# LN roots and the identity matrix moved between engines, and chord sets halved, in an attention and gated-MLP kernel

## The chip, the cores and the metric

One core of a Trainium2 chip runs the whole program. The metric is the time of one execution on the device in microseconds (us), lower is better. A unit in this text is one block of 128 x 512 attention scores; there are 2048.

In the profile PE is TensorE, PEld its weight loads, DVE is VectorE, ACT is ScalarE, POOL is GpSimd. "L1233" is line 1233 of that kernel's source; the line numbers of two kernels differ.

## The reference, cut to what matters

```python
B, S, D, H, F = 1, 2048, 512, 32, 1792
def _layernorm(x): return (x - mean(x)) / sqrt(var(x) + 1e-5)
def _A(x):                                   # attention, 32 heads of 16
    q, k, v = split(x @ wqkv)
    p = softmax(einsum("bhqd,bhkd->bhqk", q, k) / 4)
    return merge(einsum("bhqk,bhkd->bhqd", p, v)) @ wo
def _B(x): return (sigmoid(x @ w_gate) * (x @ w_up)) @ w_down
h = x + _A(_layernorm(x))                    # LN1
out = h + _B(_layernorm(h))                  # LN2
```

## The kernel before

The instruction order of every engine is fixed when the kernel is built. A Python scheduler keeps a model clock for each engine, with assumed durations, and places each piece of work where the model says that it is ready. The rows of x come in 16 tiles of 128, in four chunks of four. Layer normalization needs the reciprocal root of each row's variance, called *root* here; GpSimd takes it with its power operation. The first exps start as soon as chunk 0 is through LN1 and its projections; the other twelve row tiles and the dense projections run beside the attention.

A score tile has three units (two in the first stretch). ACT computes exp on two of them; the third can be taken by DVE, which writes an int16 approximation of the exp's bits. That one needs two more int16 copies, shifted by a constant (the *chords*), and all three are multiplied with V. So a split moves one unit's exp from ACT to DVE, and costs PE two more products with V (*value products*). The chords are int16 additions packed four to a 64-bit word, which GpSimd does. Units of DVE are collected in a set, in one buffer J of three planes: set size `GQ`, buffers `QB`. Sets of four are called quads below, sets of two pairs.

```python
nc.vector.memset(eps_t[:], 1e-5)
nc.scalar.activation(out=A0[:], in_=eps_t[:], func=ACT.Exp)       # loads the exp table
nc.vector.memset(fill[:], 1.0)
make_identity(nc, ident_bf[:])                                    # memset and select on GpSimd
nc.gpsimd.memset(Vaug[:, :, :, DH:VW], 0.5)                       # the sum column of V
... mask, ident2, maskz from ident_bf, on VectorE ...

def rstd_of(dst, var, eps=1e-5):                                  # LN1, every row tile
    v = small.tile([P, 1], FP32, name="nv")
    nc.gpsimd.tensor_scalar(out=v[:], in0=var, scalar1=eps, scalar2=None, op0=ALU.add)
    nc.gpsimd.tensor_tensor(out=dst, in0=v[:], in1=power[:], op=ALU.pow)

def early_ln(c):                                                  # chunks 1 to 3
    for i in range(TQ):
        j = ... statistics of the row tile, on VectorE ...
        j = rstd_job(rstds[c][:, i:i + 1], mvs[c][:, i, 1:2], j)  # on GpSimd
        ja.append(dve(325, lambda i=i: apply(c, i), j, ...))
    ...

GQ, QB = 4, 3
def dexp_rest():                                                  # a set is full, or its group ends
    ...
    for s in (1, 2):                                              # two chords of the k units
        gq.append(Job(150 + 192 * k, lambda s=s: chord64(s), ...))

# a tile is split only if VectorE is free in time and a buffer is
split = (dable and max(T["D"], sc_end[n] + LAT) <= start + 600
         and (half or len(quads) < QB) and pend <= 2600)
```

## Time and profile before

| | before |
|---|---|
| median of the runs before the prediction | 788.99 us (787.13 to 789.88) |
| first exp of scores starts | 21.2 us |
| units on VectorE | 579 |
| exps of three units on ACT (tiles not split) | 85 |
| GpSimd's 64-bit adds | 340, 308 us |

The head of the page: busy us, share of the span, instructions; then the chain of waits by engine.

```profile
PE 745.8 (95%) x11460; PEld 351.4 (45%) x11460; DVE 606.0 (77%) x1194; ACT 724.2 (92%) x780; POOL 324.2 (41%) x379
...
PE 68%; DVE 15%; ACT 11%; issue 4%; POOL 2%; DVEq 0%; POOLq 0%; ACTq 0%
```

The windows of the kernel before, without that of 80 to 160 us: from and to in us, length, then busy us and number of instructions of PE, PEld, DVE, ACT and POOL, granted PE clock, DMA share, GB/s.

```profile
0.00:21.20 21.20, 11.14 (x68) 6.69 (x69) 8.50 (x25) 4.76 (x11) 6.08 (x15) 0.76 0.67 210
21.20:80.00 58.80, 56.08 (x402) 17.68 (x400) 50.21 (x106) 54.01 (x56) 18.03 (x34) 1.00 0.00 1
160.00:740.00 580.00, 563.72 (x9608) 276.66 (x9606) 462.12 (x911) 566.67 (x600) 257.35 (x287) 1.00 0.18 51
```

From 160 to 740 us, PE and ACT are both busy for 97 to 98% of the time. In the first 21 us no engine is busy for much more than half of the time.

The chain of waits in the first 22 us: start, length, what.

```profile
0.99 8.15 issue
9.14 0.29 POOL ident_bf masks.py:199
...
9.74 1.95 DVE ident L257
```

The 8.15 us of "issue", time in which nothing that the profile shows is waited for, lie in GpSimd's own queue, in front of the select that makes the identity. Then a VectorE instruction of 128 columns takes 1.95 us, while GpSimd fills the column of Vaug. What sits in the 8 us can be read from the view of that source line: duration min/median/max in ns, then first and last start.

```profile
masks.py:199 POOLq MODIFY_POOL_CONFIG  x2: 11/11/11, 0.9 to 1.0; - x2
...
masks.py:199 POOL TENSOR_SCALAR_AFFINE_SELECT ident_bf<-ident_bf x1: 282/282/282, 9.1 to 9.1; 128x128 bf16<-128x128 bf16 x1
```

A second such configuration stands before the first 64-bit add, at 45.3 us; the first add runs at 51.2:

```profile
L1260 POOL INT64_ADD J<-J x340: 392/1037/1252, 51.2 to 750.8; - x170
...
L1260 POOLq MODIFY_POOL_CONFIG  x2: 11/11/11, 45.3 to 45.4; - x2
```

Groups by form of the kernel before (busy us, mean ns | idle before, releasers). A two-unit exp takes 1067 ns, a three-unit one 1499; the last line is the most frequent of the four three-unit forms (85 in all).

```profile
L1394 ACT ACTIVATE pt<-PS 128x1024 f16<-128x1024 f32 x450 | 444.3, 1067 | 16.0 <-PE PS L1062 13.7 <-ACT pt L1394 0.2
L1233 DVE TENSOR_SCALAR J<-PS 128x512 int16<-128x512 f32 x579 | 384.8, 681 | 105.4 <-PE PS L1210 50.5 <-PE PS L1062 36.7 <-ACT pt L1394 11.3
L1260 POOL INT64_ADD J<-J x340 | 308.4, 920 | 398.3 <-DVE J L1233 357.5 <-DVE rsum L1098 24.5 <-DVE nt L287 7.7
...
L1394 ACT ACTIVATE pt<-PS 128x1536 f16<-128x1536 f32 x68 | 99.5, 1499 | 3.5 <-PE PS L1210 1.1 <-PE PS L1062 1.0 <-ACT pt L1394 0.9
```

Such exps come in clumps. The timeline around 371 us, first ACT, then DVE (start, length, instruction, idle before):

```profile
370.74 5.98 ACT L1394 ACTIVATE pt<-PS 128x1536 f16<-128x1536 f32 x5
```

```profile
370.18 0.68 DVE L1233 TENSOR_SCALAR J<-PS 128x512 int16<-128x512 f32 x1
375.37 0.69 DVE L1233 TENSOR_SCALAR J<-PS 128x512 int16<-128x512 f32 x1 [4.52 <-PE PS L1210]
```

VectorE idles for 4.5 us while ACT does all three units of five tiles. What it then waits for are value products on PE (L1210), which free a buffer.

### The profile page before, as it was taken

Reading aid. Unit: us, or ns where it says so; the run is one execution under the profiler, and the core shown is the slowest. Engines: PE = TensorE matmul, PEld = TensorE weight load, DVE = VectorE, ACT = ScalarE, POOL = GpSimd, SP = SyncE. Lnnn points to the kernel's source line nnn. Section 1 sums busy time; section 2 is a strip of 40 time slices with the busy share of each in tenths; the row PEclk is TensorE's granted clock in tenths of the full one; section 3 lists DMA queues with packets and bytes.
Section 4 is the critical chain, followed back from the end, with each engine's and each line's share of the span. In section 5 each row is a group of like instructions: output and inputs, shape, how many; then the busy total and the mean of one; then the engine's idle time right before and its main releaser. Section 6 shows DMA issues by size and latency. Waiting matters only on the chain.

```text
span 786.9 us, 26382 instructions
## 1 busy us (share of the span) xinstructions
PE 745.8 (95%) x11460; PEld 351.4 (45%) x11460; DVE 606.0 (77%) x1194; ACT 724.2 (92%) x780; POOL 324.2 (41%) x379
## 2 busy tenths in 40 slices
PE   5999998999999999999999999999999999999997
PEld 2322223444454445543444445443554455445554
DVE  3996987888978797787799666885879767967743
ACT  2989988999999999998999999999999999999962
POOL 3331444555543535344355434443444434443510
PEclk7999999999999999999999999999999999999999
DMA  7000005000023103200110203111221123102260
GB/s 227 1 1 1 2 1 162 3 2 3 3 82 96 35 9 96 83 28 9 50 56 29 83 27 96 44 31 40 70 82 29 36 77 116 34 16 82 59 199 17
DMA packets 66809, 41.59 MB, mean 53 GB/s; under 512 B 3456, under 2 KB 66688, under 8 KB 66688
## 3 DMA queue, kind: packets, MB, share of 16 engines
q1 hardware_dynamic: 66400, 39.59, 17.0%
q8 instruction: 91, 1.49, 0.8%
q14 instruction: 30, 0.25, 0.1%
q10 hardware_dynamic: 288, 0.26, 0.1%
HBM read 37.75 MB, written 2.10 MB: 51 GB/s over the span
## 4 chain that ended last, share of the span: by engine, by line
PE 68%; DVE 15%; ACT 11%; issue 4%; POOL 2%; DVEq 0%; POOLq 0%; ACTq 0%
PE PS L1210 22%; PE PS L1062 21%; PE PS L801 12%; ACT pt L1394 8%; PE PS L819 6%; DVE J L1233 6%; PE PS L309 3%; POOL J L1260 2%; PE PS L740 2%; DVE xs L1128 1%; DVE st L261 1%; ACT xnT L1394 1%; PE PS L314 1%; PE PS L1541 1%; DVE Vaug L318 1%
## 5 line engine op out<-in xcount | busy, mean ns | idle before, releaser
L1394 ACT ACTIVATE pt<-PS 128x1024 f16<-128x1024 f32 (+1 forms) x519 | 536.0, 1123 | 19.5 <-PE PS L1062 14.7
L1260 POOL INT64_ADD J<-J x340 | 308.4, 920 | 398.3 <-DVE J L1233 357.5
L1233 DVE TENSOR_SCALAR J<-PS 128x512 int16<-128x512 f32 x579 | 384.8, 681 | 105.4 <-PE PS L1210 50.5
L1062 PE MATMUL PS<-QT,KT 32*128 32x256 bf16 (+1 forms) x3712 | 266.4, 276 | 8.7 <-ACT pt L1394 3.7
L1210 PE MATMUL PS<-J,Vaug 128*17 128x256 f16 (+1 forms) x3315 | 240.3, 280 | 4.9 <-POOL J L1260 2.1
L1210 PE MATMUL PS<-pt,Vaug 128*17 128x256 f16 (+1 forms) x2107 | 207.0, 280 | 3.3 <-DVE xs L1128 2.3
L1210 PEld LDWEIGHTS <-Vaug 128*17 128x17 bf16 x6050 | 138.0, 90 | 107.5 <-issue 99.2
L1062 PEld LDWEIGHTS <-KT 32*128 32x128 bf16 x3840 | 91.8, 92 | 196.5 <-issue 192.6
L801 PE MATMUL PS<-xnT,wgu 128*128 128x256 bf16 x784 | 113.7, 275 | 1.7 <-DVE h L769 0.8
L1394 ACT ACTIVATE xnT<-PS 128x1024 f16<-128x1024 f32 (+1 forms) x87 | 96.5, 1138 | 1.7 <-PE PS L1062 1.5
L801 PEld LDWEIGHTS <-wgu 128*128 128x128 bf16 x784 | 63.8, 97 | 41.1 <-issue 35.8
L819 PE MATMUL PS<-wd,hT 128*128 128x512 bf16 x196 | 56.5, 383 | 0.0
L1210 PE MATMUL PS<-xnT,Vaug 128*17 128x256 f16 x368 | 54.6, 274 | 0.0
L1394 ACT ACTIVATE QTb<-PS 128x1024 f16<-128x1024 f32 x41 | 44.4, 1082 | 0.7 <-PE PS L1062 0.6
L831 ACT ACTIVATE th<-PS 128x512 f32<-128x512 f32 (+1 forms) x63 | 37.4, 594 | 7.5 <-DVE hT L814 6.1
L873 DVE SCALAR_TENSOR_TENSOR hT<-th,PS 128x512 bf16<-128x512 f32 x49 | 33.3, 680 | 12.9 <-PE PS L801 11.8
L1128 DVE STREAM_TRANSPOSE xs<-PS 128x256 f32<-128x256 f32 (+1 forms) x60 | 27.6, 461 | 13.6 <-PE PS L1210 13.1
L1210 PE MATMUL PS<-QTb,Vaug 128*17 128x256 f16 (+1 forms) x162 | 28.0, 278 | 0.7 <-DVE xs L1128 0.7
L1099 DVE TENSOR_TENSOR o<-xs,rsum 128x128 bf16<-128x128 f32 (+1 forms) x60 | 26.1, 435 | 2.1
L1394 ACT ACTIVATE xb<-PS 128x1024 f16<-128x1024 f32 (+2 forms) x25 | 25.9, 1082 | 1.5 <-PE PS L1062 1.5
L1394 ACT ACTIVATE pe<-PS 128x1024 f16<-128x1024 f32 (+1 forms) x22 | 22.2, 1090 | 0.5 <-PE PS L1062 0.4
L819 PEld LDWEIGHTS <-hT 128*128 128x128 bf16 x196 | 12.6, 97 | 20.9 <-issue 16.9
(118 smaller groups left out, 416.9 us busy)
## 6 DMA issues: line engine op xcount, KB each, us to landing
wgu<-in_B_w_gate_dram SPq DMA_DIRECT2D x49, 256.0 KB, 3.0
wgu<-in_B_w_up_dram SPq DMA_DIRECT2D x49, 256.0 KB, 3.4
out_dram<-ob SPq DMA_DIRECT2D x16, 128.0 KB, 1.7
wd<-in_B_w_down_dram SPq DMA_DIRECT2D x1, 1792.0 KB, 7.8
xr<-in_A_x_dram SPq DMA_DIRECT2D x14, 128.0 KB, 3.8
xb<-in_A_x_dram SPq DMA_DIRECT2D x6, 256.0 KB, 6.8
J<-in_B_w_gate_dram SPq DMA_DIRECT2D x2, 768.0 KB, 4.9
J<-in_B_w_up_dram SPq DMA_DIRECT2D x2, 768.0 KB, 6.6
```

The source lines that it names most:

```text
L309: nc.tensor.matmul(ps, lhsT=w_sb[:, d, p * P:(p + 1) * P], rhs=xnT[c][:, d, :], start=(d == 0), stop=(d == DC - 1))
L801: nc.tensor.matmul(ps[:, 0:PARTS[r][2]], lhsT=w[:, d, :], rhs=hn_of(r)[:, d, :], start=(d == 0), stop=(d == DC - 1))
L819: nc.tensor.matmul(ps, lhsT=hT[:, f, i * P:(i + 1) * P], rhs=wd[:, f, :], start=(f == 0), stop=(f == FC - 1))
L831: nc.scalar.activation(out=th[:, 0:ps.shape[-1]], in_=ps, func=ACT.Tanh, scale=0.5)
L873: nc.vector.scalar_tensor_tensor(out=hT[:, f:f + k, 0:w], in0=th[f][:].rearrange("p (k n) -> p k n", k=k), scalar=1.0, in1=ps2.rearrange(" ...
L1062: nc.tensor.matmul(pss[:, ui, i * CW[qc]:(i + 1) * CW[qc]], lhsT=KT[g // 2][32 * j:32 * j + 32, k * P:(k + 1) * P], rhs=q[32 * j:32 * j + ...
L1099: nc.vector.tensor_tensor(out=o2[:, 0:w // 32, DH * a:DH * a + DH], in0=xs[:, 0:w // 32, 0:DH], in1=rec.to_broadcast([P, w // 32, DH]), op ...
L1128: j = dve(650 - ns[0], lambda: nc.vector.transpose(out=xs[:, 0:w // 32, :].rearrange("p b r -> p (b r)"), in_=src), Mark(T["P"] + DRAIN), ...
L1210: nc.tensor.matmul(dst[32 * j:32 * j + VW, 0:w], lhsT=un.v[:, kt * SPAN[qc] + i, h, :], rhs=un.ap[:, i * w:(i + 1) * w], start=clears and ...
L1233: nc.vector.tensor_scalar(out=J[:, 0, k, :], in0=src, scalar1=ZOFF, scalar2=float(-min(CHORDS)), op0=ALU.add, op1=ALU.max)
L1260: nc.gpsimd.int64_add(words(s), words(0), CHORDS[s - 1] * (1 + 2 ** 16 + 2 ** 32 + 2 ** 48))
L1394: ex = nc.scalar.activation(out=pt, in_=pss[:, 0:wa, :], func=ACT.Exp, scale=AS)
```

## The change

The intent: take GpSimd off the way to the first exp and leave it one sort of work, 64-bit adds. The identity is made on VectorE. The roots of chunk 0 are taken by ACT with its square root and inverted by VectorE (then ACT must load the exp table). The roots of chunks 1 to 3 are Newton runs on VectorE (a first guess and two refining steps), one per chunk of four row tiles. The chord sets become pairs, with six buffers in the same bytes. With pairs the tail's weights take five J buffers instead of three. The diff, cut to its core:

```diff
-    nc.scalar.activation(out=A0[:], in_=eps_t[:], func=ACT.Exp)
+    nc.scalar.activation(out=A0[:], in_=eps_t[:], func=ACT.Sqrt)
...
-    make_identity(nc, ident_bf[:])
+    nc.vector.memset(ramp[:, 0, 0:1], 0.0)
+    for k in (1, 2, 4, 8, 16):
+        nc.vector.tensor_scalar(out=ramp[:, 0, k:2 * k], in0=ramp[:, 0, 0:k], scalar1=float(k), scalar2=None,
+                                op0=ALU.add)
+    nc.vector.transpose(out=ramp[:, 1, :], in_=ramp[:, 0, :])
+    nc.vector.memset(ident_bf[:], 0.0)
+    nc.vector.tensor_tensor(out=ramp[:, 2, :], in0=ramp[:, 0, :], in1=ramp[:, 1, :], op=ALU.is_equal)
+    for b in range(0, P, 32):
+        nc.vector.tensor_copy(out=ident_bf[b:b + 32, b:b + 32], in_=ramp[b:b + 32, 2, :])
...
-        Task(("r", 0, i), [("f", 0, i)], [("G", 750, lambda i=i: rstd_of(
-            rstds[0][:, i:i + 1], mvs[0][:, i, 1:2]))])
+        Task(("q", 0, i), [("f", 0, i)], [("A", 270, lambda i=i: root(i))])
+        Task(("r", 0, i), [("q", 0, i)], [("D", 200, lambda i=i: V.reciprocal(
+            out=rstds[0][:, i:i + 1], in_=rstds[0][:, i:i + 1]))])
...
-    TINY = 330.0
+    TINY = 400.0
...
-            j = rstd_job(rstds[c][:, i:i + 1], mvs[c][:, i, 1:2], j)
-            ja.append(dve(325, lambda i=i: apply(c, i), j, After(("x", c - 1, i // 2)), pr=pr))
+            js.append(j)
+        for ns, part in zip((230.0, 330.0, 330.0), rstd_steps(rstds[c][:], mvs[c][:, :, 1])):
+            js = [dve(ns, part, *js, pr=pr)]
+        for i in range(TQ):
+            ja.append(dve(325, lambda i=i: apply(c, i), js[0], After(("x", c - 1, i // 2)), pr=pr))
...
-    GQ, QB = 4, 3
+    GQ, QB = 2, 6
```

Cut: Newton on several columns (a first guess of two instructions and two steps of three), the removal of a way to do chords on VectorE that the trace of before never used, the move of `fill` and `eps4_t` to GpSimd, the task that loads the exp table after the roots of chunk 0, and the start of VectorE's model clock (2900 instead of 2600 ns). `TINY` is the assumed duration of a Newton step of LN2.

More of the change, by code (lines that the diff above doesn't have):

```diff
@@ L7 @@
 from concourse._compat import with_exitstack
-from concourse.masks import make_identity
 FP32 = mybir.dt.float32
@@ L206 @@
     maskz = const.tile([P, 2], FP32)
-    power = const.tile([P, 1], FP32)
     xnT = [const.tile([P, DC, QC], BF16, name=f"xnT{c}") for c in range(NQC)]
@@ L247 @@
     nc.vector.memset(eps_t[:], 1e-5)
-    nc.scalar.activation(out=A0[:], in_=eps_t[:], func=ACT.Exp)
+    nc.scalar.activation(out=A0[:], in_=eps_t[:], func=ACT.Sqrt)
     fill = prep.tile([P, QC], BF16, name="fill")
-    nc.vector.memset(fill[:], 1.0)
-    make_identity(nc, ident_bf[:])
+    nc.gpsimd.memset(fill[:], 1.0)
     nc.gpsimd.memset(Vaug[:, :, :, DH:VW], 0.5)
-    nc.vector.memset(eps4_t[:], 4e-5)
-    nc.vector.memset(power[:], -0.5)
-    nc.vector.tensor_reduce(out=mask[:], in_=ident_bf[:].rearrange("p (b a d) -> p a b d", a=2, d=DH),
-                            axis=AX.XY, op=ALU.max)
+    nc.gpsimd.memset(eps4_t[:], 4e-5)
+    ramp = prep.tile([P, 3, 32], BF16, name="ramp")
+    nc.vector.memset(ramp[:, 0, 0:1], 0.0)
[7 more added lines that the diff above has]
+        nc.vector.tensor_copy(out=ident_bf[b:b + 32, b:b + 32], in_=ramp[b:b + 32, 2, :])
+    nc.vector.tensor_reduce(out=mask[:], in_=ramp[:, 2, :].rearrange("p (a d) -> p a d", a=2),
+                            axis=AX.X, op=ALU.max)
     nc.vector.tensor_scalar(out=ident2[:], in0=ident_bf[:], scalar1=2.0, scalar2=None, op0=ALU.mult)
@@ L264, in stats2 @@
         nc.vector.bn_aggr(out=mv, in_=st[:])
-    def rstd_of(dst, var, eps=1e-5):
-        v = small.tile([P, 1], FP32, name="nv")
-        nc.gpsimd.tensor_scalar(out=v[:], in0=var, scalar1=eps, scalar2=None, op0=ALU.add)
-        nc.gpsimd.tensor_tensor(out=dst, in0=v[:], in1=power[:], op=ALU.pow)
     def rstd_steps(dst, var):
-        v = small.tile([P, 1], FP32, name="nv")
-        y = [small.tile([P, 1], FP32, name=f"ny{i}") for i in range(2)] + [dst]
-        t = small.tile([P, 1], FP32, name="nt")
+        n = dst.shape[-1]
@@ L278, in rstd_steps @@
+        v, y0, y1, t = (small.tile([P, TQ], FP32, name=f"nw{i}")[:, 0:n] for i in range(4))
         scale = 2.0 ** (-4 / 9)
         def guess():
-            nc.vector.tensor_scalar(out=v[:], in0=var, scalar1=1e-5, scalar2=None, op0=ALU.add)
-            nc.vector.tensor_scalar(out=y[0][:].bitcast(I32), in0=v[:].bitcast(I32), scalar1=-0.5,
+            nc.vector.tensor_scalar(out=v, in0=var, scalar1=1e-5, scalar2=None, op0=ALU.add)
+            nc.vector.tensor_scalar(out=y0.bitcast(I32), in0=v.bitcast(I32), scalar1=-0.5,
@@ L283, in guess, with newton @@
                                     scalar2=1597463007.0 - 4 / 9 * 2 ** 23, op0=ALU.mult, op1=ALU.add)
-        def newton(i, s):
-            src, out = y[i][:], (y[i + 1][:] if i == 0 else dst)
-            nc.vector.tensor_scalar(out=t[:], in0=src, scalar1=src, scalar2=v[:], op0=ALU.mult, op1=ALU.mult)
-            nc.vector.tensor_scalar(out=out, in0=t[:], scalar1=3 * s * s, scalar2=src,
-                                    op0=ALU.subtract, op1=ALU.mult)
-        return guess, lambda: newton(0, scale), lambda: newton(1, -2 * scale ** 3)
+        def newton(src, out, s):
+            if n == 1:
+                nc.vector.tensor_scalar(out=t, in0=src, scalar1=src, scalar2=v, op0=ALU.mult, op1=ALU.mult)
+                nc.vector.tensor_scalar(out=out, in0=t, scalar1=3 * s * s, scalar2=src,
+                                        op0=ALU.subtract, op1=ALU.mult)
+            else:
+                nc.vector.tensor_tensor(out=t, in0=src, in1=src, op=ALU.mult)
+                nc.vector.tensor_tensor(out=t, in0=t, in1=v, op=ALU.mult)
+                nc.vector.scalar_tensor_tensor(out=out, in0=t, scalar=3 * s * s, in1=src,
+                                               op0=ALU.subtract, op1=ALU.mult)
@@ L292, in new_st @@
+        return guess, lambda: newton(y0, y1, scale), lambda: newton(y1, dst, -2 * scale ** 3)
     def new_st():
@@ L376, in fix, with root @@
             V.tensor_tensor(out=mv[:, 1:2], in0=mv[:, 1:2], in1=t[:], op=ALU.subtract)
+    def root(i):
+        A.activation(out=rstds[0][:, i:i + 1], in_=mvs[0][:, i, 1:2], func=ACT.Sqrt, bias=eps_t[:, 0:1])
     def apply(c, i):
@@ L436 @@
                                        ("D", 400, lambda h=h: keys0(h, False))], frees=h)
-    Task("go", [("qt", 0), ("qt", 1), ("kt", 0)], [])
+    Task("exps", [("q", 0, i) for i in range(TQ)], [("A", 1500, lambda: A.activation(
+        out=small.tile([P, 1], FP32, name="warm")[:], in_=eps_t[:], func=ACT.Exp))])
+    Task("go", [("qt", 0), ("qt", 1), ("kt", 0), "exps"], [])
     succ = {n: [] for n in tasks}
@@ L450, in rank_of @@
         return rank[n]
-    free = {"P": 1300.0, "A": 3200.0, "D": 2600.0, "G": 3600.0, "N": 0.0}
+    free = {"P": 1300.0, "A": 3200.0, "D": 2900.0, "G": 3600.0, "N": 0.0}
     WARM = 4800.0
@@ L535, in end @@
             return None if self.job.end is None else self.job.end + self.ns
-    dq, aq, gq, chain = [], [], [], deque()
+    dq, aq, gq = [], [], []
     def run_pool():
@@ L543, in run_pool @@
                 job.place("G")
-    def rstd_job(dst, var, *deps):
-        st["pows"] += 1
-        def power():
-            st["pows"] -= 1
-            rstd_of(dst, var)
-        gq.append(Job(800, power, deps))
-        job = gq[-1]
-        run_pool()
-        return job
-    TINY = 330.0
+    TINY = 400.0
     st = {"n": 0, "cur": 0, "pm": None, "mark": None, "acc": [None, None], "left": 0.0, "mode": None,
-          "R": 3, "ring": -1, "pms": [], "acts": deque(), "open": None, "item": None, "xs": None, "pows": 0, "on_pool": False}
+          "R": 3, "ring": -1, "pms": [], "acts": deque(), "open": None, "item": None, "xs": None}
     def dve(ns, fn, *deps, pr=0):
@@ L571, in act @@
         return aq[-1]
-    def pop_chain():
-        ns, f = chain.popleft()
-        T["D"] += ns
-        f()
     def run_dve(until, slack=450.0):
@@ L588, in run_dve @@
             else:
-                if chain and T["D"] + chain[0][0] <= until + slack:
-                    pop_chain()
-                    continue
                 if first is not None and T["D"] < first < until:
@@ L672, in early_ln @@
         pr = 2 * (c - 1)
-        ja = []
+        ja, js = [], []
         for i in range(TQ):
@@ L1248, in dexp_rest @@
         k = len(quad)
-        def chord(s):
-            nc.vector.tensor_scalar(out=J[:, s, 0:k, :], in0=J[:, 0, 0:k, :], scalar1=float(CHORDS[s - 1]),
-                                    scalar2=0.0, op0=ALU.add, op1=ALU.max)
-            for i in range(k):
-                quad[i][s].end = T["D"] + TAIL["D"]
         def words(s):
@@ L1262, in chord64 @@
                 quad[i][s].end = T["G"] + TAIL["G"]
-        st["on_pool"] = st["on_pool"] or started() and not st["pows"]
         for s in (1, 2):
-            if st["on_pool"]:
-                gq.append(Job(150 + 192 * k, lambda s=s: chord64(s), [Mark(T["D"] + TAIL["D"])]))
-            else:
-                chain.append((70 + 133 * k, lambda s=s: chord(s)))
+            gq.append(Job(150 + 192 * k, lambda s=s: chord64(s), [Mark(T["D"] + TAIL["D"])]))
         run_pool()
-    def pop_chain():
-        ns, f = chain.popleft()
-        T["D"] += ns
-        f()
-    def started():
-        return all(("ap", c) in done for c in range(1, NQC))
     def want_dve(n):
@@ L1283, in want_dve @@
             return False
-        pend = sum(c[0] for c in chain)
         busy = sum(j.ns for j in dq if j.ready() is not None)
@@ L1288, in want_dve @@
             return False
-        if pend > 2600 or busy > 1500:
+        if busy > 1500:
             return False
-        return pend + busy + 1900 + 1100 * (GQ - len(half[1:])) <= rest * 1100
+        return busy + 1900 + 1100 * (GQ - len(half[1:])) <= rest * 1100
     class Slot:
@@ L1333, in p_slots @@
                 continue
-            if half and not chain:
+            if half:
                 dexp_rest()
-            if chain:
-                pop_chain()
     lns = {c: early_ln(c) for c in range(1, NQC)}
@@ L1377 @@
         busy = sum(j.ns for j in dq if j.ready() is not None)
-        pend = sum(c[0] for c in chain)
         dable = len(tl) > 1 and busy <= 1500
-        split = (dable and max(T["D"], sc_end[n] + LAT) <= start + 600 and (half or len(quads) < QB)
-                 and pend <= 2600)
+        split = (dable and max(T["D"], sc_end[n] + LAT) <= start + 600 and bool(half or len(quads) < QB))
         if n > N - 12:
-            end = max(T["D"], sc_end[n] + LAT) + pend + 1900 + 600 * (GQ - len(half[1:]) if half else GQ)
+            end = max(T["D"], sc_end[n] + LAT) + 1900 + 600 * (GQ - len(half[1:]) if half else GQ)
             split = split and end <= start + 1330 * (N - n) - 500
@@ L1436 @@
                 flush()
-                if not av(8, 1e12):
-                    pop_chain()
+                if not av(8, 1e12) and half:
+                    dexp_rest()
             slots[:] = [s for s in slots if not s.early]
@@ L1449 @@
         dexp_rest()
-    while chain:
-        pop_chain()
     flush()
```

## The prediction

> **What bounds it now.** The windows view gives, for 160 to 740 us, PE busy 563.7 of 580 us (97%), ACT 566.7 (98%), DVE 80%, POOL 44%. Each score tile (3 units of 512 columns) is read by a two-unit exp on ACT (1067 ns) and one unit on DVE; when DVE doesn't take it, ACT does three units (about 1500 ns). The groups by form show 579 DVE units and 85 three-unit exps, which come in clumps. At 371 to 376 us the timeline shows five of them while DVE sits idle: the chord buffers are held by units whose value matmuls PE hasn't done. A split costs PE two more value matmuls, so three-unit exps are how the schedule balances two full engines.
>
> At the start, the chain of waits opens with 8.15 us of "issue": GpSimd's select for the identity starts only at 9.14 us and DVE waits for it, then again until 11.65 us while GpSimd fills Vaug (2.25 us); GpSimd's powers (0.26 + 0.59 us each) gate the LN rows. The first exp starts at 21.2 us.
>
> **What the change does.**
> 1. Identity on DVE: about 16 tiny instructions of 0.06 to 0.27 us (as such ones last in the trace), 2.5 us from 0.8 us on. GpSimd's fills (0.6 + 2.25 us) run beside them and may hold them as before. Statistics start at 5 to 6 us (x landed at 3.7); the first row's end near 6.5 instead of 11.7: minus 5 us.
> 2. Roots on ACT (0.2 to 0.3 us plus a 0.17 us reciprocal) replace powers: minus 0.5 us or more. A second table load (1.28 us) before the first exp has time; at most 0.5 us shows. First exp at about 15 us: minus 6, kept to the end, as PE and ACT are near full after it.
> 3. LN1 rows 4 to 15: powers leave POOL; three batched Newton runs come to DVE, about 1 us each. DVE is 85% busy from 21 to 80 us: 0 to 1 us lost.
> 4. Chords by pairs, same buffer bytes. A four-unit add took about 1.04 us, a two-unit one about 0.6, so POOL's adds rise from 308 to about 350 us, under half the span. The second chord comes 1.2 instead of 2.06 us after its last unit. On the chain of waits POOL adds hold ten places, 16.9 us, shrinking to some 10. Buffers recycle sooner: 50 to 75 three-unit exps, ACT minus 10 us, PE plus 2 to 4. As PE is as full as ACT, I count 5 us.
> 5. Tail: ten weight loads instead of six into the J buffers; nothing.
>
> The Trainium skill, "GPSIMD Engine Reference", section "Instruction dispatch", states about 6 us for the first call of a freshly loaded kernel. The trace has 8.2 us before the first select, and a gap of 6.04 us between the last power and the first 64-bit add, put down to DVE. Afterwards the first add may pay that; six pair buffers cover most.
>
> **Prediction:** 788.99 - 6 (start) - 5 (pairs) + 0.5 (DVE) = 778 us, 768 to 785. Faster by over 2%: 0.27; within 2%: 0.69; slower: 0.04.
>
> **Would show it right:** first exp at 14 to 16.5 us, no 8 us issue at the head of the chain; pair adds near 0.6 us, total 340 to 360; fewer three-unit exps; POOL's share of the chain below 2%.
>
> **Would make it wrong:** DVE's setup held by GpSimd's fills past 6 us; a load of 6 to 8 us before the first add with matmuls waiting; a static schedule out of step with the chip, since it is laid out from assumed durations (0.534 us for a pair add); or PE less full than its busy share says, when more splits would give 15 us.

## The result, and the profile after

| | before | after |
|---|---|---|
| median, 4 runs each | 788.06 us (787.10 to 789.88) | 776.97 us (776.81 to 777.90) |
| ratio | | 0.9859 (0.9836 to 0.9882) |
| first exp of scores | 21.2 us | 16.05 us |
| units on VectorE / three-unit exps | 579 / 85 | 616 / 47 |
| 64-bit adds | 340, 308 us | 648, 378 us |

A ratio in this text is the mean time of one kernel's fast runs over that of the other's of the same rounds, so not quite the ratio of the medians quoted. The 1.4% is clear of noise and under 2%. The total fell where the prediction put it, at 778. The parts didn't.

Page and windows of the kernel after, again without 80 to 160 us:

```profile
PE 742.5 (96%) x11614; PEld 350.2 (45%) x11614; DVE 634.3 (82%) x1270; ACT 709.9 (91%) x787; POOL 381.2 (49%) x655
...
PE 73%; DVE 15%; ACT 7%; issue 3%; POOL 1%; DVEq 0%; ACTq 0%; POOLq 0%
```

```profile
0.00:21.20 21.20, 15.94 (x94) 7.84 (x94) 16.15 (x52) 12.03 (x21) 2.97 (x7) 0.92 0.66 211
21.20:80.00 58.80, 51.28 (x363) 15.98 (x362) 49.01 (x119) 47.39 (x51) 12.63 (x22) 0.97 0.00 1
160.00:740.00 580.00, 571.46 (x9961) 281.79 (x9954) 493.68 (x959) 565.62 (x616) 325.24 (x559) 1.00 0.18 51
```

The first window shows the gain of the start: ACT did 12.0 us of work in it, not 4.8. The second gives it back: ACT did 47.4 instead of 54.0 us of work, PE 51.3 instead of 56.1. No engine is full in that window any more. Whom ACT waits for there, in the kernel before from 21 to 80 us and after from 16 to 80 us (total us, times, longest):

```profile
ACT pt L1394 <- PE PS L1062: 2.1, 7, 0.6
ACT xb L1394 <- PE PS L1062: 1.2, 1, 1.2
```

```profile
ACT pe L1366 <- PE PS L1057: 5.8, 5, 2.0
ACT pt L1366 <- PE PS L1057: 4.8, 5, 2.0
```

ACT waits 10.6 us for scores that PE makes late, against 3.3.

Counting units in the timeline by the end of their exp gives the progress of both, after minus before: -5.2 us when 32 units are done (31.7 against 36.9 us), -1.5 at 64, +0.9 at 128, **+4.6 at 256** (130.0 against 125.4), -0.8 at 900, -13.1 at the last. So the gain of the start was spent by 128 units, the kernel then ran behind the one before, and the whole of what was won in the end was won after 256 units.

The chain of waits at the start of the kernel after:

```profile
1.32 2.22 DVE ramp L254
...
8.64 1.28 ACT L446
```

The 8 us are gone from the chain. One 2.2 us instruction among tiny ones stands in it, and the load of the exp table.

The groups by form of the kernel after:

```profile
L1366 ACT ACTIVATE pt<-PS 128x1024 f16<-128x1024 f32 x474 | 460.9, 1073 | 11.4 <-PE PS L1057 9.5 <-PE PS L1205 0.4 <-ACT pt L1366 0.3
L1228 DVE TENSOR_SCALAR J<-PS 128x512 int16<-128x512 f32 x616 | 411.4, 682 | 77.9 <-PE PS L1057 43.4 <-PE PS L1205 22.1 <-POOL J L1249 5.3
L1249 POOL INT64_ADD J<-J x648 | 378.2, 596 | 356.1 <-DVE J L1228 276.0 <-DVE nw L291 43.2 <-DVE rsum L1093 17.8
L1366 ACT ACTIVATE pt<-PS 128x1536 f16<-128x1536 f32 x37 | 53.4, 1460 | 10.0 <-PE PS L1205 4.5 <-PE PS L1057 3.1 <-DVE ob L820 1.0
```

And the first chunk and the last chunk of Newton on VectorE, from the timeline (`nw` is Newton, `xn` the normalized row tile):

```profile
23.67 0.16 DVE L281 TENSOR_SCALAR nw<-mv 128x4 f32<-128x4 f32 x1
...
27.28 1.35 DVE L388 TENSOR_SCALAR xn<-xb,mv,rstd 128x512 bf16<-128x512 bf16 x4
...
44.60 0.16 DVE L281 TENSOR_SCALAR nw<-mv 128x4 f32<-128x4 f32 x1
...
49.18 1.38 DVE L388 TENSOR_SCALAR xn<-xb,mv,rstd 128x512 bf16<-128x512 bf16 x4
```

Each run has eight instructions of 0.13 to 0.46 us, 4.1 us in all for the three chunks. But from its first instruction to the first normalized row tile 3.6 and 4.6 us pass, because other work stands between the steps in VectorE's queue, and no row of a chunk may go before all four are ready. The twelve row tiles are done at 50.6 us, though this kernel started 5 us sooner than the one before, where they were done at 45.7 us.

### The profile page after: what moved, and what is told of

Its sections match the earlier page's. It is cut to its first block, busy times and chain, and to the rows that moved or that the text cites. A ratio compares the mean times of both kernels' runs of the same rounds, so it can differ in the third digit from the quotient of the medians.

```text
span 776.0 us, 27196 instructions
## 1 busy us (share of the span) xinstructions
PE 742.5 (96%) x11614; PEld 350.2 (45%) x11614; DVE 634.3 (82%) x1270; ACT 709.9 (91%) x787; POOL 381.2 (49%) x655
## 4 chain that ended last, share of the span: by engine, by line
PE 73%; DVE 15%; ACT 7%; issue 3%; POOL 1%; DVEq 0%; ACTq 0%; POOLq 0%
PE PS L1057 23%; PE PS L1205 22%; PE PS L796 14%; DVE J L1228 6%; ACT pt L1366 6%; PE PS L814 5%; PE PS L314 3%; PE PS L735 2%; DVE st L267 1%; DVE Vaug L323 1%; PE PS L319 1%; POOL J L1249 1%; PE PS L1511 1%; DVE xs L1123 1%; PE PS L308 1%
## 5 line engine op out<-in xcount | busy, mean ns | idle before, releaser
L1249 POOL INT64_ADD J<-J x648 | 378.2, 596 | 356.1 <-DVE J L1228 276.0
L1366 ACT ACTIVATE pt<-PS 128x1024 f16<-128x1024 f32 (+1 forms) x515 | 513.2, 1097 | 22.7 <-PE PS L1057 13.9
L1228 DVE TENSOR_SCALAR J<-PS 128x512 int16<-128x512 f32 x616 | 411.4, 682 | 77.9 <-PE PS L1057 43.4
L1205 PE MATMUL PS<-J,Vaug 128*17 128x256 f16 (+1 forms) x3534 | 243.6, 279 | 3.1 <-DVE xs L1123 1.5
L1205 PE MATMUL PS<-pt,Vaug 128*17 128x256 f16 (+1 forms) x2029 | 201.3, 279 | 2.2 <-DVE xs L1123 2.0
L1057 PEld LDWEIGHTS <-KT 32*128 32x128 bf16 x3840 | 89.2, 92 | 198.6 <-issue 192.5
L1366 ACT ACTIVATE xnT<-PS 128x1024 f16<-128x1024 f32 (+1 forms) x89 | 94.6, 1086 | 0.6 <-PE PS L1057 0.4
L1123 DVE STREAM_TRANSPOSE xs<-PS 128x256 f32<-128x256 f32 (+1 forms) x60 | 27.7, 462 | 12.2 <-PE PS L1205 11.5
L1366 ACT ACTIVATE xb<-PS 128x1024 f16<-128x1024 f32 (+2 forms) x28 | 28.1, 1043 | 1.5 <-PE PS L1057 1.2
L1366 ACT ACTIVATE pe<-PS 128x1024 f16<-128x1024 f32 (+1 forms) x22 | 22.9, 1067 | 5.9 <-PE PS L1057 5.8
```

The costliest lines, as they stand in the source:

```text
L1057: nc.tensor.matmul(pss[:, ui, i * CW[qc]:(i + 1) * CW[qc]], lhsT=KT[g // 2][32 * j:32 * j + 32, k * P:(k + 1) * P], rhs=q[32 * j:32 * j + ...
L1123: j = dve(650 - ns[0], lambda: nc.vector.transpose(out=xs[:, 0:w // 32, :].rearrange("p b r -> p (b r)"), in_=src), Mark(T["P"] + DRAIN), ...
L1205: nc.tensor.matmul(dst[32 * j:32 * j + VW, 0:w], lhsT=un.v[:, kt * SPAN[qc] + i, h, :], rhs=un.ap[:, i * w:(i + 1) * w], start=clears and ...
L1228: nc.vector.tensor_scalar(out=J[:, 0, k, :], in0=src, scalar1=ZOFF, scalar2=float(-min(CHORDS)), op0=ALU.add, op1=ALU.max)
L1249: nc.gpsimd.int64_add(words(s), words(0), CHORDS[s - 1] * (1 + 2 ** 16 + 2 ** 32 + 2 ** 48))
L1366: ex = nc.scalar.activation(out=pt, in_=pss[:, 0:wa, :], func=ACT.Exp, scale=AS)
```

## The experiments

Twelve runs. All outputs are right. The kernel before took 787.2 to 787.6 us beside them (medians; its single runs 786.7 to 791.4). By the rule of 2%, after, e1_start, e4_two and f1_lim3 are "same", e7_powq is "unclear" (its four runs spread from 768.0 to 772.6 us), and all others are faster. The medians:

| run | start | roots of chunks 1 to 3 | chord sets | us | ratio to before |
|---|---|---|---|---|---|
| before | old | GpSimd power, by row tile | 4 x 3 | 787.4 | 1 |
| e2_pairs | old | GpSimd power, by row tile | 2 x 6 | 767.3 | 0.9733 |
| e1_start | new | Newton, by four | 4 x 3 | 776.0 | 0.985 |
| after | new | Newton, by four | 2 x 6 | 777.0 | 0.9859 |
| e4_two | new | Newton, by two | 2 x 6 | 784.5 | 0.9957 |
| e7_powq | new | GpSimd power, by row tile | 4 x 3 | 768.4 | 0.9768 |
| e3_pow | new | GpSimd power, by row tile | 2 x 6 | 757.3 | 0.9615 |
| e6_pow4 | new | GpSimd power, by four | 2 x 6 | 765.8 | 0.9721 |
| e9_tiny | as e3_pow, `TINY` back at 330 | | 2 x 6 | 760.7 | 0.9655 |
| e8_fill | as e3_pow, Vaug's column on ACT | | 2 x 6 | **753.5** | **0.9567** |
| f1_lim3 | as e8_fill | | 2 x 6, three in use | 783.4 | 0.9941 |
| f2_q3 | as e8_fill | | 3 x 4 | 765.5 | 0.9718 |
| f3_ns | as e8_fill, pair add assumed 604 ns | | 2 x 6 | 756.3 | 0.9603 |
| g1_room7 | as e8_fill, 6 exp slots less | | 2 x 7 | 763.1 | 0.9692 |

### e1_start and e2_pairs: each half alone

```diff
# e1_start, on the changed kernel          # e2_pairs, on the kernel before
-    GQ, QB = 2, 6                         -    GQ, QB = 4, 3
+    GQ, QB = 4, 3                         +    GQ, QB = 2, 6
```

> The new start alone: the changed kernel with sets of four and three buffers. Theory (the start's 5.1 us are eaten again before 256 score units are done, because all four rows of an LN1 chunk now wait for one batched Newton run; the pairs give the whole gain): first exp near 16 us, but 256 units done no earlier than the kernel before (125 us or later), and a time of 786 to 791 us. Rival (the record: start worth 6 us, pairs worth 5): a time near 782.5 us, 256 units done near 120 us.

> The pairs alone: the kernel before with two-unit chord sets and six buffers, its start untouched. Theory (pairs give 11 us or more, the start nothing in the end): first exp at 21.2 us, three-unit exps about 45 to 55 instead of 85, pair adds near 0.6 us, a time of 772 to 778 us. Rival (pairs worth 5): 783 to 785 us.

Measured: 776.0 and 767.3 us. The pairs alone are worth 20 us, four times what the prediction gave them, and e2_pairs is faster than the whole change. But my theory for e1_start fell: the start with Newton and quads isn't worth nothing, it is worth 11.4 us, about as much as the whole change. Its 256 units were done at 124.8 us, as early as in the kernel before (125.4), as the theory said; its gain came after that, which the theory didn't say. Both halves are worth more than 11 us, and together they are worth 11. One of them spoils the other, and in the stretch up to 80 us, where the first traces point, the candidates are few.

### e3_pow and e4_two: where the roots of chunks 1 to 3 are taken

```diff
# e3_pow, on the changed kernel (cut: rstd_of and its constant, as in the kernel before)
-            js.append(j)
-        for ns, part in zip((230.0, 330.0, 330.0), rstd_steps(rstds[c][:], mvs[c][:, :, 1])):
-            js = [dve(ns, part, *js, pr=pr)]
-        for i in range(TQ):
-            ja.append(dve(325, lambda i=i: apply(c, i), js[0], After(("x", c - 1, i // 2)), pr=pr))
+            gq.append(Job(800, lambda i=i: rstd_of(rstds[c][:, i:i + 1], mvs[c][:, i, 1:2]), [j]))
+            j = gq[-1]
+            run_pool()
+            ja.append(dve(325, lambda i=i: apply(c, i), j, After(("x", c - 1, i // 2)), pr=pr))
# e4_two, on the changed kernel, simplified: the same Newton run after every second row tile
+            if i % 2 < 1:
+                continue
+            a = i - 1
+            for ns, part in zip((230.0, 330.0, 330.0),
+                                rstd_steps(rstds[c][:, a:i + 1], mvs[c][:, a:i + 1, 1])):
+                js = [dve(ns, part, *js, pr=pr)]
+            for r in range(a, i + 1):
+                ja.append(dve(325, lambda r=r: apply(c, r), js[0], After(("x", c - 1, r // 2)), pr=pr))
+            js = []
```

> The changed kernel with the roots of rows 4 to 15 on GpSimd by its power again, row by row, the identity staying on VectorE. Theory: rows come as early as in the kernel before minus about 5 us, and the time falls to 771 to 775 us. It also tells where the 8 us before GpSimd's first select belong: if to any GpSimd instruction beyond a fill, the first add or power starts about 8 us late or after a hidden load in the first 11 us; if to the select alone, nothing. If the switch from power to 64-bit add costs about 6 us each time, the gap between the last power and the first add is 6 us again, and the gain is lost where adds and powers mix.

> The changed kernel with the Newton runs of rows 4 to 15 done by two rows instead of four (six runs instead of three, about 3 us more of VectorE work). Theory (the batch of four holds the rows): normalized rows 5 to 16 come 3 to 6 us earlier than the changed kernel's 27.7 to 50.6 us, ScalarE's waits on TensorE between 21 and 80 us shrink from about 10 us, and the time falls by 3 to 5 us to 772 to 774. Rival (the early stretch is held by VectorE's total work or by the loads, not by the batch): 777 us or slower.

Measured: 757.3 us, 19.7 us less than the changed kernel, and 784.5, 7.5 us more. So it is the Newton runs that spoil the change, by far more than I had expected. But the batch isn't the whole reason: with runs of two the first two row tiles came at 22.7 and 23.1 us instead of 27.7, the last ones at 54.3 and 54.6, later than with runs of four. Twice as many small instructions went through VectorE's queue. (Some of e4_two's loss may be the PE clock. It was granted at half speed for 6.8 us from 31 us on and for 13.7 us from 55 us on; in the kernel after there were two spells of 3.4 us, from 12.1 and 32.5 us on. What this cost wasn't taken apart.)

The timelines of e3_pow show the last row tiles on VectorE, then the last power and the first adds on GpSimd:

```profile
40.17 0.73 DVE L395 TENSOR_SCALAR xn<-xb,mv,rstd 128x512 bf16<-128x512 bf16 x2
```

```profile
39.73 0.57 POOL L277 TENSOR_TENSOR rstd<-fix,power 128x1 f32<-128x1 f32 x1
46.33 4.33 POOL L1255 INT64_ADD J<-J  x8 [6.03 <-DVE J L1234]
```

The rows are done at 40.9 us, 9.7 us sooner than with Newton. The gap between power and add is 6.03 us, as it was 6.04 before. The profile puts it down to VectorE, whose unit came at 46.0 us. But the configuration stands in GpSimd's queue at 40.5 us, 5.8 us before the first add, and then eight adds follow without a pause: sets had piled up. Of the ten other traces with powers ahead of the adds, nine have 5.6 to 5.8 us there and f1_lim3 has 6.1; in e6_pow4 the wait is put down to "issue". So GpSimd pays for the switch from powers to 64-bit adds, and in the changed kernel it doesn't, as the configuration then stands at 3.2 us. That was the intent of leaving GpSimd one sort of work. It is worth little: the first set waits 2.7 us (its second unit was done at 43.6 us), while the Newton runs that replaced the powers cost 19.7.

The 8 us at the start of the kernel before stand behind a configuration as well. In e3_pow the first configuration stands at 3.2 us and the first power runs at 18.1 us, as soon as its row is ready, so there the load lay under other work. Why 8.2 us there and 5.8 later wasn't tried.

### e6_pow4 and e7_powq: waiting or instructions; do the parts add up?

```diff
# e6_pow4, on e3_pow, cut: one power for a chunk, after its four statistics
-            gq.append(Job(800, lambda i=i: rstd_of(rstds[c][:, i:i + 1], mvs[c][:, i, 1:2]), [j]))
+            js.append(j)
+        gq.append(Job(800, lambda: rstd_of(rstds[c][:], mvs[c][:, :, 1]), js))
# e7_powq, on e3_pow
-    GQ, QB = 2, 6
+    GQ, QB = 4, 3
```

> The power variant (757.3 us, against 777.0 of the changed kernel), but with one power for all four rows of an LN1 chunk, so that a chunk's rows wait for each other as they do for the batched Newton run, while VectorE gets no extra instruction. Theory A (the eight tiny Newton instructions per chunk on VectorE cost the time): 755 to 761 us. Theory B (waiting for all four rows costs it): 768 to 778 us, rows 13 to 16 normalized at about 48 us instead of 35 to 41.

> The power variant with chord sets of four and three buffers: new start without Newton and without pairs. If the parts add up as the other runs suggest (start minus 10, pairs minus 20): 776 to 779 us, and then the Newton runs cost nothing beside quads (the new start with Newton and quads took 776.0). If Newton costs about 20 us whatever the chord sets, this run must come to 756 to 760 us, and pairs would be worth nothing beside the new start.

Measured for e6_pow4: 765.8 us, between the two theories. Of the 19.7 us of Newton, 8.4 (757.3 to 765.8) come with the wait for all four rows alone, and 11.2 (765.8 to 777.0) with moving the work into VectorE's queue. (Both are above the 3 to 4 us that a mere reordering may do; see e9_tiny.) The last rows of chunk 3 stood at 45.1 us: 40.9, 45.1 and 50.6 us in the three kernels, in the order of the times.

```profile
38.38 1.04 POOL L277 TENSOR_TENSOR rstd<-nw,power 128x4 f32<-128x4 f32 x1
```

(The power of four columns takes 1.04 us, that of one 0.57, so this run asks less of GpSimd than e3_pow.)

Measured for e7_powq: 768.4 us, outside both guesses. The parts don't add up: Newton costs 7.6 us with quads (776.0 to 768.4) and 19.7 with pairs; pairs are worth 20.1 us on the old start, 11.1 on the new one with powers, and nothing with Newton. Each unit's end, counted as above, tells where. Up to 256 units the four kernels with the new start need 119.2 us (powers, quads), 116.6 (powers, pairs), 124.8 (Newton, quads), 130.0 (Newton, pairs). So in that stretch Newton costs 5.6 us with quads and 13.4 with pairs. After it, the times to the last unit are 613.4, 604.2, 615.3 and 608.8 us: there the pairs are worth 9.2 us with powers and 6.5 with Newton. Why Newton and pairs hurt each other before 256 units isn't shown; both bring small work into the same stretch of VectorE's and GpSimd's queues, but no run took that apart. The kernel before needs 626.5 us for that stretch and e2_pairs 606.3.

### e8_fill and e9_tiny: what holds VectorE's setup; what a constant of the schedule does

```diff
# e8_fill, on e3_pow, cut
-    nc.gpsimd.memset(Vaug[:, :, :, DH:VW], 0.5)
+    def fill_v():                              # called after ACT's second copy of chunk 0
+        A.activation(out=Vaug[:, :, :, DH:VW], in_=fill[:].rearrange("p (t h o) -> p t h o", t=NT, h=H),
+                     func=ACT.Copy, scale=0.5)
# e9_tiny, on e3_pow
-    TINY = 400.0
+    TINY = 330.0
```

> The power variant with the constant column of Vaug written by ScalarE after its second copy instead of by GpSimd at 1.2 us. Theory (GpSimd's fill of 2.3 us holds VectorE's third ramp instruction, which took 2.2 us): VectorE's setup ends near 3.5 us instead of 5.4, the first exp comes 1.0 to 1.8 us earlier than 16.0 to 17.2 us, and the time falls by 1 to 2 us. Rival (the ramp's wait is something else): setup and first exp unchanged.

> The power variant with the schedule's assumed duration of a small VectorE step back at 330 ns from 400. It does the same work; only the order shifts. If that constant matters, the new one was part of the gain: 760 us or more. If not, the difference to 757.3 us shows how far the time moves by a mere reshuffling; I expect 3 us or less.

Measured for e8_fill: 753.5 us, and the first exp at 12.98 us. The five ramp instructions in the kernel after and in e8_fill, and GpSimd's fill beside those of the kernel after:

```profile
0.93 3.02 DVE L254 TENSOR_SCALAR ramp<-ramp 128x1 bf16<-128x1 bf16 x5
1.19 2.32 POOL L249 MEMSET Vaug<- 128x512 bf16 x1
```

```profile
0.93 1.03 DVE L255 TENSOR_SCALAR ramp<-ramp 128x1 bf16<-128x1 bf16 x5
```

With the fill gone from GpSimd the ramp takes 1.03 us and the statistics begin at 3.48 us instead of 5.47. The Trainium skill says in "GPSIMD Engine Reference", section "Specifications", that GpSimd shares its SBUF interfaces with VectorE, with contention for VectorE instructions in a two-port performance mode or with two SBUF inputs. This pair of traces shows the contention: the third ramp instruction, of 4 elements, stood until the fill ended at 3.5 us. Whether it meets the page's condition they don't tell: it has one input in SBUF, and no view shows whether it ran in a two-port mode. The gain of the run is 3.8 us, more than the 2 us of the setup and more than I expected. In e3_pow's profiled run the PE clock stood at one half for 6.8 us from 11.6 us on, and its first exp came at 16.8 us; six other kernels with this start had it at 15.1 to 16.1. But that doesn't explain the rest: two other runs of e3_pow, at a mean clock of 0.996 and 0.997 against 0.993, took the same 757.3 us. What is left is below the size of a mere reordering, which the next run measures.

Measured for e9_tiny: 760.7 us, 3.4 more than e3_pow, for one assumed duration of a small step. I take 3 to 4 us as the size below which a difference between two of these static schedules may be nothing but order. The run gives a cleaner worth of the start, too: e2_pairs and e9_tiny have the same constant, the same powers for chunks 1 to 3 and the same sets, and differ by 6.6 us (767.3 and 760.7). And it names a part of what isn't explained: the kernel before and e2_pairs have the old constant, e1_start and e7_powq the new one, and no run has the old start with quads and the new constant.

### f1_lim3, f2_q3, f3_ns and g1_room7: why pairs help, and whether more is to be had

```diff
# f1_lim3, on e8_fill, in the three places that ask for a free buffer
-        if not half and len(quads) >= QB:
+        if not half and len(quads) >= 3:
# f2_q3                                    # f3_ns
-    GQ, QB = 2, 6                         -  gq.append(Job(150 + 192 * k, ...
+    GQ, QB = 3, 4                         +  gq.append(Job(170 + 217 * k, ...
# g1_room7
-    GQ, QB = 2, 6                         -    NPT, NPE = 24, 14
+    GQ, QB = 2, 7                         +    NPT, NPE = 18, 14
```

> The power variant with the moved Vaug fill (753.5 us), where only three of the six pair buffers may be in use at once, so six units are held instead of twelve: sets of two with half the room. If the pairs gain because sets are small (a chord comes sooner, a buffer is free sooner): 753 to 757 us and 50 to 65 three-unit exps. If they gain by room alone (buffers in use longer than the schedule allows): 765 us or more and over 100 three-unit exps.

> The same with sets of three and four buffers, twelve units of room. If the gain grows as the set shrinks (quads 11 us slower than pairs on the power variant): between, 756 to 762 us, with 60 to 75 three-unit exps. If order alone decides, anything from 750 to 765 us without a matching count of three-unit exps.

> The same as the moved-fill variant, with the schedule's assumed duration of a pair add set from 534 ns to 604 ns, near the measured 596. If the mismatch costs anything: 749 to 752 us. If not, the same work in a slightly different order: 751 to 757 us, and it shows again how far a reshuffling moves the time.

> The moved-fill power variant (753.5 us) with seven pair buffers instead of six, paid for with six of the 24 slots that hold ScalarE's exps, so the bytes are the same. Three buffers in use took 783.4 us with 139 three-unit exps, six took 753.5 with 54. If room for chords still limits: fewer than 45 three-unit exps and 745 to 752 us. If ScalarE's slots are as scarce, or the count of three-unit exps is now set by VectorE's other work: 753 to 760 us.

Measured, with the count of three-unit exps: e8_fill 753.5 us and 54; sets of three 765.5 and 69; three pair buffers in use 783.4 and 139; seven pair buffers 763.1 and 33. f1_lim3 met the guess for room alone, f2_q3 its count but not its time, and g1_room7 neither of its guesses for the time. Groups by form and head of the page, first of f1_lim3, then of e8_fill:

```profile
L1383 ACT ACTIVATE pt<-PS 128x1536 f16<-128x1536 f32 x118 | 175.5, 1527 | 3.2 <-PE PS L1074 1.0 <-PE PS L1222 0.9 <-ACT pt L1383 0.3
PE 731.6 (94%) x11190; PEld 350.5 (45%) x11273; DVE 572.9 (73%) x1154; ACT 747.0 (96%) x786; POOL 333.6 (43%) x583
```

```profile
L1383 ACT ACTIVATE pt<-PS 128x1536 f16<-128x1536 f32 x46 | 67.6, 1480 | 3.2 <-PE PS L1222 1.2 <-ACT pt L1383 1.0 <-ACT xb L1383 1.0
PE 717.5 (95%) x11506; PEld 347.3 (46%) x11587; DVE 622.4 (83%) x1242; ACT 711.3 (95%) x786; POOL 385.7 (51%) x675
```

Room and set size both matter, and I take it for the same reason: a tile is split only if a buffer is free. With half the room 85 more exps have three units. At 432 ns each (1499 - 1067 ns, from the profile of before) that is 37 us more work for ACT; the time rose by 29.9 us. From 54 to 69 it is an estimated 6.5 us, of 12.0 measured. The pages show the same from both sides. ACT was busy 35.7 us longer in f1_lim3. By the pages' counts PE executed 316 fewer matmuls there, waited 16.1 us for exps (`pt`) instead of 5.3, and was yet busy 14.1 us longer, so its busy time says little of its room. So in this pair the time follows ACT's work, and PE has room for the value products of more splits. This is what the prediction denied.

But the count of three-unit exps doesn't rule alone. g1_room7 has the fewest and is 9.6 us slower. Its exp slots were cut to pay for the buffer, and its waits show it: ACT waited 5.8 us on nothing but "issue" ahead of exps and 5.3 us for value products, against 1.2 us for value products in e8_fill. That the slots did it is argued, not shown.

f3_ns: 756.3 us. An assumed duration near the measured one (596 ns) made nothing faster; the 2.8 us are again of the size of a mere reordering.

## Why the prediction was right, point by point

The time was right, 777.0 against 778, and the range held it. That was luck: in the order below it missed 15 us of the gain of the pairs, 4 of the start and 19 of the cost of Newton, and these errors cancel. In one order that the runs allow, 787.4 -> 767.3 (pairs) -> 757.3 (start, with the new constant) -> 777.0 (Newton):

| term | predicted | measured |
|---|---|---|
| 1, 2: identity, roots of chunk 0 | -6 | -10.0, of which -3.4 with the constant; -6.6 with equal constants (-19.0 beside quads, with the new constant) |
| 4: pairs | -5 | -20.1 on the old start (-11.1 on the new one with powers, +1.0 beside Newton) |
| 3: Newton for chunks 1 to 3, and "a table load" | +0.5 | +19.7 (+7.6 beside quads) |

*The start.* The mechanism was right, and beside pairs the size, too. Beside quads the start with powers gained 19.0 us (787.4 to 768.4), of which 6.2 by 256 units; the rest came later and isn't explained by an earlier first exp. The first exp came at 16.05 us, in the 14 to 16.5 foretold; the 8 us of issue left the chain; GpSimd's fill held VectorE's setup, as the prediction feared, until 3.5 us, which e8_fill showed by taking it away. But "kept to the end" was wrong for this change: it was gone by 128 units. A part of the earlier exp may be the PE clock: it stood at one half for 10.2 us from 8.8 us on in the kernel before and for 3.4 us in the kernel after. With the new start and no such spell the first exp came at 15.1 us, with 3.4 us of it at 16.05, with 6.8 at 16.8; that is about 0.25 us per us of half clock, and for the 6.8 us of difference an estimated 1.7 of the 5.1 us.

*Newton.* The failed step is the third: "three batched Newton runs come to DVE, about 1 us each. DVE is 85% busy from 21 to 80 us: 0 to 1 us lost." The instructions' own time was near enough, 4.1 us for all three. What wasn't in the sum is that the runs stand at the head of everything that the early stretch needs: rows, then keys and values of a chunk, then scores. The step counted busy time where it should have followed when the row tiles come out. That time went from 40.9 to 50.6 us, by waiting for four rows (8.4 us of the total) and by steps that queue behind VectorE's other work (11.2 us). And it took GpSimd's slower but free hands away: an addition and a power take 0.26 + 0.59 us there, but need not queue behind other work.

The Trainium skill's "GPSIMD Engine Reference", section "Engine selection", sends elementwise additions, products and maxima to VectorE, as GpSimd is about half as fast with two inputs. No run here takes a power on VectorE, but the durations point the same way (0.59 us for one power of one column, 0.13 to 0.17 us for most Newton instructions of four). A power isn't among the operations that it names, and for the roots its choice doesn't hold here: on GpSimd row by row they made the kernel 19.7 us faster than Newton by four, and by four still 11.2.

*Pairs.* The adds' duration was right (596 ns against 0.6), their total a little over the 340 to 360 foretold (378 us), and POOL's share of the chain fell from 2% to 1%. The three-unit exps fell to 47 (55 in e2_pairs), where 50 to 75 were foretold. The step that failed is "As PE is as full as ACT, I count 5 us." PE's busy share of 97% isn't a share of its capacity. With pairs and powers PE did the value products of about 30 more splits and the time still fell by 11 to 20 us, and in f1_lim3 the time followed ACT's work. The prediction named this in its last paragraph as what would give 15 us, and then didn't believe it.

*GpSimd's load.* The skill's "GPSIMD Engine Reference", section "Instruction dispatch", states about 6 us for the first call of a freshly loaded kernel. The runs agree: 5.6 to 5.8 us from the configuration to the first add in ten of the eleven traces where powers went before; the 8.2 us before the first select are more. The fear that the first add would pay it after the change was wrong: the load stood at 3.2 us and was hidden.

What stays open: why Newton costs 12 us more beside pairs than beside quads (7.8 of it before 256 units, by the profiled runs); why quads with the old start and the old constant take 11 to 13 us longer after 256 units than quads with the new ones; why seven buffers lose.

The best kernel that these runs found is e8_fill: new start, pairs, powers on GpSimd for chunks 1 to 3, the column of Vaug on ACT. It takes 753.5 us, 4.3% less than the kernel before and, by the medians, 3.0% less than the change.

## What to carry to other kernels

Cost a move between engines by when its result comes out at the head of the chain, not by the busy time it adds; four microseconds of small steps, batched by four rows in a contended queue, cost 8 to 20 us here, and a slower engine that was free did better. When a bundle of changes moves the time as foretold, undo its parts one by one all the same: this one held a part that was worth 20 us and one that cost as much. Two engines that are both 97% busy needn't be equally scarce; give the one less work, as f1_lim3 did in reverse, and see which of them the time follows.

## What the Trainium skill lacked or had wrong

- "GPSIMD Engine Reference", section "Instruction dispatch", gives the load as about 6 us, at the first call of a freshly loaded kernel, "with no visible profile instruction". Here 8.2 us pass ahead of the first select at the start, and 5.6 to 5.8 us between the configuration and the first 64-bit add in ten of eleven traces. A configuration, the instruction from which the page itself measures, does stand in the trace of GpSimd's sequencer, with the source line of the operation that follows. The page doesn't say which operations share a load: in the kernel before none stands between the select, the fill and the powers, and one between the powers and the 64-bit adds. One that stands early in the queue is hidden, as at 3.2 us in the changed kernel.
- No page has a duration for a power or a 64-bit add on GpSimd: 0.57 us for a power of one column and 1.04 for four, 596 ns mean for a pair add (1024 int16 per partition), 1037 ns median for the sets of up to four.
- No page has a duration for a fill on GpSimd: 512 elements with a stride took 2.3 us, 512 without one 0.53 us. The strided fill took as long on ACT (2.39 us), where VectorE's setup didn't wait for it.
- "ScalarE: Activation LUTs", section "What ACT_TABLE_LOAD costs", counts 1283 ns for a load and about 1380 ns for a drain. The load took 1.28 us here, and no drain shows: it began 0.02 us after the last root, and the next activation 0.02 us after it.
